# A weight load cut by rows: one 128-row transfer becomes four of 96, 25, 5 and 2 rows

## The chip, the core and the metric

The kernel runs on one core of a Trainium2 chip. The metric is the device time of one execution in microseconds (us), the median of several. The core has a matrix engine (TensorE, PE; its weight loads are shown as PEld), VectorE (DVE), ScalarE (ACT), GpSimd (POOL), SyncE (SP, which here only issues transfers and waits), and sixteen DMA engines that move data between the chip's main memory and the on-chip memory of 128 rows (partitions).

## The reference

One decoding step for 8 sequences, all in float32. `x` (8 by 512) is layer-normalised. Attention over a cache with 32 query heads and 8 key/value heads of 128, 4096 positions each, gives `o` (8 by 4096); the output projection multiplies it with `wo` (4096 by 512). A small gated MLP on the same normalised `x` gives a gate. The result is

```
s = softmax(q k^T / sqrt(128)) v  @ wo        # 8 x 512
out = x + s * silu(mlp(xn))                   # 8 x 512
```

The key and value caches are 128 MB each; `wo` is 8 MB.

## The kernel before, in words

All large operands come in transfers of 8 MB, 128 rows of 64 KB, into three slots of on-chip memory, `slot_a`, `slot_b` and `slot_c`. Per key/value head there are four: two halves of the keys (slots a and b) and two halves of the values (slots c and b). SP issues all of them in `Heads.loads`, in the order written there, each after a wait on TensorE's progress that says the slot is free. After the last head, slot a takes `wo` instead of the next keys.

`wo` comes in seven pieces, cut along the columns of the slot (`WO_PIECES`, in units of 256 columns, 1 KB of each row). Every piece has a semaphore of its own in `landed_wo`; a transfer adds 16 to it when all of it has landed. A piece's transfer has 128 rows, one for each partition. The sixth piece, units 60 to 63, has 3 KB a row. The small table `x_out` (128 rows of 256 bytes, the residual in the output's layout) is issued last.

`last_products` is the end of TensorE's program. It multiplies the attention output of the first seven heads with their part of `wo` (line 415, 56 products into two banks, `part`). Then VectorE and ScalarE copy these partial sums to on-chip memory (`part_sb`). TensorE meanwhile multiplies two of the last head's four parts (`direct`, line 424), folds the copied sums in (line 437), and multiplies the last two parts (line 424 again), into one bank `acc`. `need(column)` places a wait for a piece ahead of the first product that reads it, in the order of the program: the fifth piece (units 56 to 60) ahead of the first products of line 424, the sixth ahead of the ones that follow line 437, the seventh (unit 63 alone) ahead of the last quarter of those. A wait takes the semaphore down again:

```
    def take(self, sem, n):
        self.nc.tensor.wait_ge(sem, n).then_inc(sem, -n)
```

Behind the last product VectorE multiplies `acc` with the gate and adds `x_out` (two operations on 128 by 64), and ScalarE's queue issues the store of the result (32 KB).

Of the kernel before, what the change touches and what calls it, by code (L numbers as in the profile page):

```python
# [10 lines left out]
P = 128  # L11
# [13 lines left out]
SLOT = HALF * UNIT  # L25
W = 64
OUT_ROWS = 2 * B
WO_PIECES = [(0, 36), (36, 46), (46, 52), (52, 56), (56, 60), (60, 63), (63, 64)]
FOLDED = HKV * REP - REP
AHEAD = FOLDED + 2  # L30
HD = 256
# [7 lines left out]
class Chip:  # L39


    def __init__(self, nc):
        self.nc = nc

        def sb(name, *shape):
            return nc.alloc_sbuf_tensor(name, list(shape), F32).ap()
# [23 lines left out]
        self.oT = sb("oT", P, HKV - 1, REP, B)  # L70
        self.oT_last = sb("oT_last", P, REP, 2, OUT_ROWS)
        self.o_sb = [sb(f"o_sb{i}", P, DH) for i in range(2)]
# [158 lines left out]
class Heads:  # L231
# [7 lines left out]
    def __init__(self, nc, t, landed_a, landed_b, stored):  # L239
# [3 lines left out]
        self.landed_a, self.landed_b, self.landed_c = landed_a, landed_b, nc.alloc_semaphore("landed_c")  # L243
        self.landed_wo = [nc.alloc_semaphore(f"landed_wo{i}") for i in range(len(WO_PIECES))]
        self.landed_x = nc.alloc_semaphore("landed_x")
# [24 lines left out]
    def loads(self, kT, v, wo, x_rows):  # L270
        sync, (a, b, c) = self.nc.sync, self.t.slots
        for h in range(HKV):
            at = h * STEPS
            if h:
                sync.wait_ge(self.pe, at - 8 + 7)
                sync.dma_start(b, kT[h, 1]).then_inc(self.landed_b, 16)
                sync.wait_ge(self.pe, at - 8 + 6)
            sync.dma_start(c, v[h, 0]).then_inc(self.landed_c, 16)
            sync.wait_ge(self.pe, at + 2)
            sync.dma_start(b, v[h, 1]).then_inc(self.landed_b, 16)  # L280
            sync.wait_ge(self.pe, at + 1)
            if h < HKV - 1:
                sync.dma_start(a, kT[h + 1, 0]).then_inc(self.landed_a, 16)
        for (lo, hi), landed in zip(WO_PIECES, self.landed_wo):
            sync.dma_start(a[:, lo * HD:hi * HD], wo[:, lo * HD:hi * HD]).then_inc(landed, 16)
        sync.dma_start(self.t.x_out, x_rows).then_inc(self.landed_x, 16)

    def head_sides(self, h):
# [103 lines left out]
    def last_products(self):  # L392
        nc, t, step = self.nc, self.t, lambda mm: mm.then_inc(self.pe, 1)
        wo_sb = t.slots[0].rearrange("p (m d) -> p m d", d=D)
        half_d = D // 2
        here = [0]
        self.idle_products()

        def need(column):
            while here[0] < len(WO_PIECES) and WO_PIECES[here[0]][0] < column:  # L400
                self.take(self.landed_wo[here[0]], 16)
                here[0] += 1

        def quarter(m, i):
            return 2 * (m % 2) + i if m >= FOLDED - 2 else m % REP

        last = {(i, quarter(m, i)): m for m in range(FOLDED) for i in range(2)}
        starts = sorted({*range(0, FOLDED, REP), *(lo // 2 for lo, _ in WO_PIECES if lo < 2 * FOLDED), FOLDED})
        for lo, hi in zip(starts, starts[1:]):
            for i in range(2):  # L410
                for m in range(lo, hi):
                    need(2 * m + 2)
                    h, r = divmod(m, REP)
                    q = quarter(m, i)
                    mm = nc.tensor.matmul(self.part[i][R * q:R * q + B, :], t.oT[:, h, r, :],
                                          wo_sb[:, m, i * half_d:(i + 1) * half_d],
                                          start=(m < REP), stop=(m == last[i, q]))
                if hi == FOLDED:
                    step(mm)

        def direct(m, a, c, stop=False):
            need(2 * m + 2 if m < HKV * REP - 1 else 2 * m + 1 + a)
            for g in range(G):
                mm = nc.tensor.matmul(t.acc[R * g:R * g + OUT_ROWS, :], t.oT_last[:, m - (HKV - 1) * REP, a, :],  # L424
                                      wo_sb[:, m, c(g):c(g) + W], start=(m == FOLDED and a == 0), stop=stop)
            return mm

        self.take(self.token, 1)
        for m in range(FOLDED, AHEAD):
            for a in range(2):  # L430
                direct(m, a, lambda g: (2 * g + a) * W)
        self.take(self.token, 1)
        self.take(self.part1, 1)
        for a in range(2):
            for g in range(G):
                c = (2 * (g % 2) + a) * W
                nc.tensor.matmul(t.acc[R * g:R * g + OUT_ROWS, :], t.pick[:, a, :OUT_ROWS],  # L437
                                 t.part_sb[g // 2][:, c:c + W], start=False, stop=False)
        for m in range(AHEAD, HKV * REP):
            for a in range(2):  # L440
                if m < HKV * REP - 1:
                    direct(m, a, lambda g: (2 * g + a) * W)
                else:
                    mm = direct(m, a, lambda g: (G * a + g) * W, a == 1)
        step(mm)
# [55 lines left out]
```

## Time and profile before

| | us |
|---|---|
| median of 3 runs (678.39 to 678.44) | 678.40 |
| the profiled execution's own time | 678.71 |
| its span, first to last instruction | 677.4 |
| TensorE busy (modelled ends) | 405.8 |
| VectorE busy | 80.0 |
| ScalarE busy | 13.8 |
| main DMA queue, share of sixteen engines' span | 99.3% |

The span is the profiled execution on the one core; its own time holds what lies around the span too. A product's end is modelled, so a busy TensorE isn't TensorE at its peak. The DMA share of a window counts packets by when they begin and can pass 1 in a short one.

### The profile page before, as it was taken

Reading aid. Unit: us, or ns where it says so; the run is one execution under the profiler, and the core shown is the slowest. Engines: PE = TensorE matmul, PEld = TensorE weight load, DVE = VectorE, ACT = ScalarE, POOL = GpSimd, SP = SyncE. Lnnn points to the kernel's source line nnn. Section 1 sums busy time; section 2 is a strip of 40 time slices with the busy share of each in tenths; the row PEclk is TensorE's granted clock in tenths of the full one; section 3 lists DMA queues with packets and bytes.
Section 4 is the critical chain, followed back from the end, with each engine's and each line's share of the span. In section 5 each row is a group of like instructions: output and inputs, shape, how many; then the busy total and the mean of one; then the engine's idle time right before and its main releaser. Section 6 shows DMA issues by size and latency. Waiting matters only on the chain. (4 is left out here: it accounts for less than half of the span.)

```text
span 677.4 us, 5930 instructions
## 1 busy us (share of the span) xinstructions
PE 405.8 (60%) x2660; PEld 133.2 (20%) x2660; DVE 80.0 (12%) x157; ACT 13.8 (2%) x28; POOL 2.8 (0%) x15
## 2 busy tenths in 40 slices
PE   0446749346875449445794349555593349655598
PEld 0112213111221113111231113111131013211134
DVE  0142021102110021102110021101100021100211
ACT  0010000000000000000000000000000000000000
POOL 1000000000000000000000000000000000000000
PEclk9986869787896669788796779877696788976699
DMA  9999999999999999999999999999999999999997
GB/s 379 443 433 434 434 434 433 434 433 433 433 433 433 433 433 433 433 433 433 433 433 433 433 433 433 433 433 433 433 433 433 433 433 433 433 433 433 433 444 304
DMA packets 6213, 290.89 MB, mean 429 GB/s; under 512 B 952, under 2 KB 1080, under 8 KB 1600
## 3 DMA queue, kind: packets, MB, share of 16 engines
q1 hardware_dynamic: 6064, 290.79, 99.3%
q8 instruction: 4, 0.07, 0.0%
q10 hardware_dynamic: 144, 0.03, 0.0%
q14 instruction: 1, 0.01, 0.0%
HBM read 290.78 MB, written 0.03 MB: 429 GB/s over the span
## 5 line engine op out<-in xcount | busy, mean ns | idle before, releaser
L358 PE MATMUL sc<-slot_b,q 128*32 128x512 f32 x512 | 72.8, 733 | 75.8 <-PEq L340 75.8
L358 PE MATMUL sc<-slot_a,q 128*32 128x512 f32 x512 | 71.8, 724 | 72.4 <-PEq L340 72.4
L380 PE MATMUL o_ps<-slot_c,pT 128*16 128x512 f32 x512 | 72.4, 729 | 50.8 <-PEq L340 50.8
L373 PE MATMUL scr<-pT,ident 128*128 128x512 f32 x176 | 77.7, 597 | 0.0
L380 PE MATMUL o_ps<-slot_b,pT 128*16 128x512 f32 x512 | 56.5, 593 | 5.0 <-PEq L340 4.9
L358 PEld LDWEIGHTS sc<-slot_b,q 128*32 128x32 f32 x512 | 20.5, 132 | 128.2 <-issue 128.2
L264 DVE TENSOR_REDUCE nm<-sc 128x1 f32<-128x1024 f32 x8 | 9.8, 1224 | 290.1 <-PE sc L358 290.1
L358 PEld LDWEIGHTS sc<-slot_a,q 128*32 128x32 f32 x512 | 19.9, 131 | 117.9 <-issue 117.9
L373 PEld LDWEIGHTS scr<-pT,ident 128*128 128x128 f32 x176 | 32.8, 190 | 45.1 <-issue 45.1
L380 PEld LDWEIGHTS o_ps<-slot_c,pT 128*16 128x16 f32 x512 | 17.2, 112 | 99.4 <-issue 99.4
L380 PEld LDWEIGHTS o_ps<-slot_b,pT 128*16 128x16 f32 x512 | 15.7, 97 | 45.0 <-issue 45.0
L264 DVE TENSOR_TENSOR p<-o_ps,diag 128x512 f32<-128x512 f32 x8 | 5.5, 691 | 124.4 <-PE o_ps L380 124.4
L295 ACT ACTIVATE p<-sc,nm 128x1024 f32<-128x1024 f32 x8 | 8.9, 1114 | 554.3 <-DVE nm L264 554.3
L264 DVE TENSOR_TENSOR o_all<-o_ps,diag 128x512 f32<-128x512 f32 x8 | 5.5, 691 | 104.6 <-PE o_ps L380 104.6
L143 PE MATMUL scr<-ident,slot_c 8*128 8x8 f32 x4 | 0.6, 254 | 25.2 <-DVE slot_c L140 25.2
L345 PE MATMUL scr<-pT,ident 128*128 128x384 f32 x36 | 13.8, 507 | 0.0
L151 PE MATMUL scr<-slot_b,xnT 128*32 128x512 f32 x64 | 9.9, 779 | 0.3 <-DVE xnT L144 0.3
L262 DVE STREAM_TRANSPOSE pT<-p 128x1024 f32<-128x1024 f32 x8 | 10.0, 1245 | 0.3
L362 PE MATMUL scr<-ident,nm 128*1 128x128 f32 x8 | 2.2, 269 | 11.9 <-PEq L340 11.9
L262 DVE TENSOR_REDUCE o_sb<-p 128x128 f32<-128x512 f32 x8 | 8.3, 1033 | 0.3
L262 DVE TENSOR_REDUCE o_sb<-o_all 128x128 f32<-128x512 f32 x8 | 8.3, 1032 | 0.3
L388 PEld LDWEIGHTS po<-fold,o_sb 128*128 128x128 f32 x32 | 4.8, 188 | 13.5 <-issue 13.5
(96 smaller groups left out, 100.3 us busy)
## 6 DMA issues: line engine op xcount, KB each, us to landing
slot_c<-in_w_mlp SPq DMA_DIRECT2D x1, 5392.0 KB, 34.0
slot_a<-in_wo SPq DMA_DIRECT2D x1, 4608.0 KB, 39.2
slot_a<-in_wo SPq DMA_DIRECT2D x1, 1280.0 KB, 41.7
slot_a<-in_wo SPq DMA_DIRECT2D x2, 512.0 KB, 44.7
slot_a<-in_wo SPq DMA_DIRECT2D x1, 768.0 KB, 43.1
slot_a<-in_wo SPq DMA_DIRECT2D x1, 384.0 KB, 45.4
slot_a<-in_kT SPq DMA_DIRECT2D x8, 48.6
slot_b<-in_kT SPq DMA_DIRECT2D x8, 31.4
```

The lines of the kernel that those rows point to most:

```text
L143: nc.tensor.transpose(pt[:, k * B:(k + 1) * B], xn[:, k * P:(k + 1) * P], t.ident[:B, :B])
L151: nc.tensor.matmul(pq[R * g:R * (g + 1), :], t.xnT[:, k, :], wq_sb[:, k, lo:lo + REP * DH], start=(k == 0), stop=(k == NK - 1))
L262: make(*args, **kw).then_inc(self.token, 1)
L264: make(*args, **kw).then_inc(self.dve, 1)
L295: nc.scalar.activation(p, t.sc.rearrange("p c s -> p (c s)"), AF.Exp, bias=t.nm, accum_out=t.l).then_inc(self.act, 1)
L345: self.nc.tensor.matmul(t.scr[1][:, :WARM], t.ident, t.pT.rearrange("p j b g r -> p (j b g r)")[:, :WARM], start=True, stop=True)
L358: mm = nc.tensor.matmul(t.sc[R * g:R * (g + 1), c, :], t.q[:, b * R:(b + 1) * R], k_sb[:, i, c, g, :], start=(b == 0), stop=(b == B - 1))
L362: step(nc.tensor.transpose(t.scr[0][:1, :P], t.nm, t.ident))
L373: nc.tensor.matmul(t.scr[1], t.ident, flat[:, :512], start=True, stop=True)
L380: mm = nc.tensor.matmul(of[R * i:R * i + G * REP, :], pT[:, j, half * HALF + i], v_sb[:, i, j], start=(j == 0), stop=(j == J - 1))
L388: mm = nc.tensor.matmul(t.po[:, half * n:(half + 1) * n], t.o_sb[half], t.fold.rearrange("p i r -> p (i r)"), start=True, stop=True)
```

## The change

The sixth piece of `wo` is issued as four transfers, over rows 0 to 96, 96 to 121, 121 to 126 and 126 to 128, all into the same columns as before and all on the same semaphore; the wait for this piece asks for 64 in place of 16. The other pieces, the order of the pieces, and everything else stay.

```
+SHARED_PIECE = 5
+SHARES = [(0, 96), (96, 121), (121, 126), (126, 128)]
...
-        for (lo, hi), landed in zip(WO_PIECES, self.landed_wo):
-            sync.dma_start(a[:, lo * HD:hi * HD], wo[:, lo * HD:hi * HD]).then_inc(landed, 16)
+        for i, ((lo, hi), landed) in enumerate(zip(WO_PIECES, self.landed_wo)):
+            for p0, p1 in SHARES if i == SHARED_PIECE else [(0, P)]:
+                sync.dma_start(a[p0:p1, lo * HD:hi * HD], wo[p0:p1, lo * HD:hi * HD]).then_inc(landed, 16)
...
-                self.take(self.landed_wo[here[0]], 16)
+                self.take(self.landed_wo[here[0]], 16 * (len(SHARES) if here[0] == SHARED_PIECE else 1))
```

## Rows read from the trace of the kernel before

**Rows 1.** The page: DMA share and rate by slices, queue's packets, MB, share.

```profile
span 677.4 us, 5930 instructions
...
DMA  9999999999999999999999999999999999999997
GB/s 379 443 433 434 434 434 433 434 433 433 433 433 433 433 433 433 433 433 433 433 433 433 433 433 433 433 433 433 433 433 433 433 433 433 433 433 433 433 444 304
...
q1 hardware_dynamic: 6064, 290.79, 99.3%
```

**Rows 2.** Timeline of SP's last issues (start us, us, instruction).

```profile
626.34 0.33 SPq L280 DMA_DIRECT2D slot_b<-in_v  x1
626.71 3.28 SPq L285 DMA_DIRECT2D slot_a<-in_wo  x7
630.03 17.23 SPq L286 DMA_DIRECT2D x_out<-in_x_rows  x1
```

**Rows 3.** DMA issues from 629.0 to 629.2 us (KB each, us to landing).

```profile
slot_a<-in_wo SPq DMA_DIRECT2D x1, 512.0 KB, 45.0
slot_a<-in_wo SPq DMA_DIRECT2D x1, 384.0 KB, 45.4
```

**Rows 4.** DMA issues of the whole span (KB each, median us to landing).

```profile
slot_a<-in_wo SPq DMA_DIRECT2D x1, 4608.0 KB, 39.2
...
slot_a<-in_wo SPq DMA_DIRECT2D x1, 128.0 KB, 45.3
x_out<-in_x_rows SPq DMA_DIRECT2D x1, 32.0 KB, 45.0
out<-gate ACTq DMA_DIRECT2D x1, 32.0 KB, 1.5
...
slot_c<-in_x SPq DMA_DIRECT2D x1, 16.0 KB
```

**Rows 5.** Timeline of the end (start us, us, engine, instruction, idle before).

```profile
673.69 0.49 PEld L424 LDWEIGHTS acc<-slot_a,oT_last 128*16 128x16 f32 x32 [0.95 <-issue]
673.72 0.64 PE L424 MATMUL acc<-slot_a,oT_last 128*16 128x64 f32 x32 [0.48 <-PEq L340]
674.11 0.30 PEld L437 LDWEIGHTS acc<-part_sb,pick 128*16 128x16 f32 x16
674.17 0.42 PE L437 MATMUL acc<-part_sb,pick 128*16 128x64 f32 x16
674.60 0.54 PEld L424 LDWEIGHTS acc<-slot_a,oT_last 128*16 128x16 f32 x32 [0.18 <-issue]
674.63 0.68 PE L424 MATMUL acc<-slot_a,oT_last 128*16 128x64 f32 x32
675.35 0.22 DVE L264 TENSOR_TENSOR gate<-acc,gate 128x64 f32<-128x64 f32 x1 [1.65 <-PE acc L424]
675.61 0.22 DVE L264 TENSOR_TENSOR gate<-gate,x_out 128x64 f32<-128x64 f32 x1
675.86 0.37 ACTq L335 DMA_DIRECT2D out<-gate  x1
```

**Rows 6.** Chain that ended last, in order of time (start us, us).

```profile
673.68 0.04 issue
673.72 0.64 PE acc L424 x32
...
674.59 0.04 issue
674.63 0.70 PE acc L424 x26
```

**Rows 7.** Windows of the end, with PEclk, DMA share and GB/s last.

```profile
672.80:673.30 0.50, 0.44 (x8) 0.00 (x0) 0.03 (x1) 0.00 (x0) 0.00 (x0) 1.00 0.84 280
673.30:673.60 0.30, 0.00 (x0) 0.00 (x0) 0.30 (x1) 0.27 (x1) 0.00 (x0) 1.00 0.38 137
673.60:674.20 0.60, 0.48 (x35) 0.51 (x39) 0.10 (x1) 0.10 (x1) 0.00 (x0) 1.00 0.28 101
674.20:674.60 0.40, 0.39 (x28) 0.22 (x17) 0.00 (x0) 0.00 (x0) 0.00 (x0) 1.00 0.13 31
674.60:675.40 0.80, 0.68 (x32) 0.53 (x32) 0.05 (x1) 0.00 (x0) 0.00 (x0) 1.00 0.00 0
```

**Rows 8.** DMA queues from 669 to 677.4 us: packets, MB, share.

```profile
q8 instruction: 1, 0.02, 0.7%
```

## The prediction

> **What bounds the kernel now.** I read the page's slices and queue lines first, then the chain of waits, the timeline of the last six microseconds, the windows of the same stretch, and last the DMA issues with their landings.
>
> The page says that the kernel lives on its loads: one queue moves 290.79 MB and its packets fill 99.3% of sixteen engines' time [rows 1]. So the body runs at the pace of the transfers, and only what comes after the last load, or an uneven end of the loads, is open. The change touches only that end.
>
> The landings follow from issue plus time to landing. SP issues the seven pieces of wo from 626.71 in 3.28 us, one each 0.474 us, and x_out at 630.03 [rows 2]. The fifth piece (512 KB) is issued at 626.71 + 4 x 0.474 = 628.61 and lands 45.0 later, at 673.6; the sixth (384 KB, the one that is cut up) at 629.08 + 45.4 = 674.5 [rows 3]; the seventh (128 KB) at 629.55 + 45.3 = 674.9; x_out at 630.03 + 45.0 = 675.0 [rows 4].
>
> TensorE shows two of these as stops. Its weight loads for the folded tail begin at 673.69, 0.1 us after the fifth piece, and those of the last 32 products at 674.60, 0.1 us after the sixth [rows 5]. The view of the chain makes the stretch from 673.72 to 675.32 look like unbroken TensorE work, with 0.04 us of "issue" in it [rows 6]. But a product's end there is modelled. The weight loads tell more: those of line 437 are over at 674.11 + 0.30 = 674.41, and the next is at 674.60 with 0.18 us of idle before it [rows 5]. **So TensorE waits 0.18 us for the piece that is changed**, and no more than that can be won by landing it sooner: ahead of it stands work that the fifth piece released, and the change doesn't touch the fifth piece.
>
> The other thing to see is why the end is ragged. The DMA share is 0.84 from 672.80 to 673.30, then 0.38, 0.28 and 0.13 until 674.60 [rows 7]. Times 16 that is 6.1, then 4.5, then 2.1 engines' worth of data. If all sixteen finished together the share would fall in one step. So some eleven engines are through at about 673.3, and four or five run on, the slowest until the landing at 674.5. After 669 one 16 KB packet of instructions passes too, on another queue [rows 8]; it takes one engine for a while, and whatever that engine owes of wo is later by that much. A landing waits for the last engine.
>
> **The change part by part.** *Three more issues on SP.* An issue takes 0.43 us and one starts each 0.474 us [rows 2]: 3 x 0.474 = 1.4 us, at about 630 us. Nothing but the seventh piece and x_out stands behind them, both due 43 us later. One stall is visible: x_out's own issue lasts 17.23 us, to 647.26 [rows 2], as if the engines' queues had to drain first. With 17 packets for this piece on the fullest engine in place of 9 (below), eight more must drain before x_out fits. The first piece of wo (4,608 KB, 36 KB a row, landing at 626.71 + 39.2 = 665.9 [rows 4]) needs 4,719 / 434 = 10.9 us at the page's 434 GB/s [rows 1], so it begins at 655; even if all eight were its rows (1.36 us each), x_out is issued by 655 + 8 x 1.36 = 665.9. Its data pass at 674.5 or so: hidden by over 8 us, and without that cover VectorE's last sum at 675.61 [rows 5] would wait for it. Bounds: 0 to 0; a loss would need over 8 us more.
>
> *The wait.* TensorE still takes one semaphore once, of 64 instead of 16; no instruction is added. Zero.
>
> *Who carries the rows.* A row of this piece costs an engine (674.5 - 673.6) / 8 = 0.11 us, since the piece lands 0.9 us behind the one before it and eight rows per engine lie between; 3 KB at 434 / 16 = 27 GB/s gives 0.113, the same. The queue's 6,064 packets [rows 1] tell how transfers are cut: 128-row ones (42 of them) in 16 equal parts with one completion each, 42 x 144 = 6,048, and the 8-row transfer of x [rows 4] leaves 16, eight rows and eight completions, so eight engines with a row each. If 25, 5 and 2 rows are cut into equal parts likewise, they go to 5, 5 and 2 engines, and 96 rows to 16 engines of six. If the small ones begin at the same engine, two engines carry 13 rows, three carry 12, eleven carry 6, in place of 8. The eleven are through 2 x 0.11 = 0.22 us sooner, the five 0.44 to 0.55 later. The trace doesn't show where 25 rows go; its bounds are sixteen engines (no shift) and one engine (below). I take five.
>
> [...]
>
> *What it is worth.* If the four or five late engines are all among the eleven, the piece lands at 674.5 - 0.22 = 674.28, TensorE could go on at 674.39, and its loads are free at 674.42: the 0.18 us are gone. The seventh piece then lands 0.22 sooner too (674.64), and the last quarter of the products, which needs it, comes at about 674.42 + 0.75 x 0.54 = 674.83. So the sum is -0.18 us against the profiled execution, whose 678.71 us hold the span of 677.4 and 1.3 around it. The median of the runs is 0.31 below that execution; the same difference gives **678.40 - 0.18 = 678.2 us**.
>
> **The rivals.** *One of the late engines is among the five.* The five then finish 0.55 later, and it is a late one that does. If it is the slowest, the piece lands at 674.5 + 0.55 = 675.05 and everything behind follows: 678.95 us. If it is one of the others, which by the fall of the share are through by about 674.2 [rows 7], it lands at 674.75: 678.65. For it: rows of views name no engine, and five of sixteen are a large part. Against: what ends last is one engine, and 11 of 16 places are outside the five. It decides from the point where a late engine that carries 12 or 13 rows was less than 0.55 us ahead of the slowest.
>
> *It doesn't do what it says*: the small transfers spread over all engines and nothing shifts. 678.4 us.
>
> *25 rows stay on one engine.* With 5 and 2 on the same, it carries 38 rows, 30 more than now: 30 x 0.11 = 3.3 us. From an engine that was through at 673.2 that is 676.5, 2.0 us later than now: 680.4 us, or 681.7 from the slowest. Against it: the 8-row transfer used as many engines as it could.
>
> *Small transfers pay a fixed cost one after the other.* The final store of 32 KB takes 1.5 us from issue to landing with nothing else in flight [rows 4]; three times that would be 4.5 us, 682.9 us. Against it: x_out, also 32 KB, lands 0.1 to 0.2 us behind the piece before it [rows 4], so behind other work that time is overlapped. [...]
>
> **How the numbers follow.** The slowest engine falls outside the five with 11/16 = 0.69 if nothing is known of its place; the other late ones take some of that away. All late engines outside the five 0.48 (678.2); nothing shifts 0.07 (678.4); a late one among the five 0.18 (678.65), or the slowest 0.20 (678.95); one engine for 25 rows 0.04; fixed costs 0.02; something that gains more 0.01. The range 678.0 to 679.1 holds the first four, 0.93. 0.2% is 1.36 us, about what a measurement of this kernel can tell from no change; the first four lie inside it on both sides, so same 0.93, slower 0.06, faster 0.01.
>
> **What would show it.** The queue has 6,064 + 5 + 5 + 2 = 6,076 packets if 25, 5 and 2 rows go to 5, 5 and 2 engines (the completions of the 96 rows stand for those of the 128), 6,064 + 1 + 5 + 2 = 6,072 if the 25 stay on one, 6,064 + 48 = 6,112 if each goes to all sixteen. The idle time ahead of the last 32 products is gone or a few hundredths if I am right; 0.4 to 0.8 us, with the share of 673.6 to 674.6 higher, if a late engine is among the five. x_out's issue ends before 666. The loads for the folded tail still begin 0.1 us behind the fifth piece, at about 673.7. I am wrong if that moves, if the body before 655 runs at another pace, or if the time leaves 678.0 to 679.1.

## The result and the profile after

The changed kernel takes 679.60 us (median of 21 runs) against 678.48 us of the kernel before (21 runs of the same sessions): the ratio is 1.0016, with an interval of 1.0009 to 1.0022, so 0.6 to 1.5 us slower. That is under the 0.2% (1.36 us) that the prediction took for what a measurement can tell from no change, though by its interval it is a real loss. It lies outside the prediction's range (678.0 to 679.1), and it moved the other way.

The page of the changed kernel, its main queue:

```profile
q1 hardware_dynamic: 6076, 290.79, 99.2%
```

6,076 packets are what 25, 5 and 2 rows on 5, 5 and 2 engines give. The rows go to as many engines as forecast; which ones, no row names.

The timeline of SP in the changed kernel, answering to [rows 2]:

```profile
626.70 14.03 SPq L288 DMA_DIRECT2D slot_a<-in_wo  x10
640.78 14.54 SPq L289 DMA_DIRECT2D x_out<-in_x_rows  x1
```

The issues of the pieces now stall too, but x_out is issued at 640.78 + 14.54 = 655.3, 17 us before the first of its packets begins (672.40, by the packet records). Nothing waits for SP.

The timeline of the end in the changed kernel, answering to [rows 5]:

```profile
674.26 0.49 PEld L427 LDWEIGHTS acc<-slot_a,oT_last 128*16 128x16 f32 x32 [1.84 <-issue]
...
675.49 0.54 PEld L427 LDWEIGHTS acc<-slot_a,oT_last 128*16 128x16 f32 x32 [0.51 <-issue]
...
676.24 0.23 DVE L266 TENSOR_TENSOR gate<-acc,gate 128x64 f32<-128x64 f32 x1 [2.87 <-PE acc L427]
```

Two stops grew. The loads that wait for the **fifth** piece, which the change leaves whole, begin at 674.26 instead of 673.69 [rows 5]: +0.57. From there to the loads that wait for the sixth it is 1.23 us instead of 0.91: +0.32. The sum, 0.89, is the whole difference of the two profiled executions (679.60 against 678.71). By the idle time in front of them (the brackets) the two stops grew by 0.89 and 0.33; the changed execution had come to this point 0.33 us earlier. Behind it everything keeps its length.

Why the fifth piece is late shows in windows of the same stretch (DMA share and GB/s are the last two columns). The changed kernel:

```profile
671.90:672.40 0.50, 0.34 (x8) 0.13 (x8) 0.00 (x0) 0.00 (x0) 0.00 (x0) 1.00 1.16 248
672.40:672.90 0.50, 0.50 (x8) 0.02 (x4) 0.00 (x0) 0.00 (x0) 0.00 (x0) 1.00 0.91 199
```

And the kernel before:

```profile
671.90:672.40 0.50, 0.35 (x5) 0.00 (x0) 0.00 (x0) 0.00 (x0) 0.00 (x0) 1.00 0.96 391
672.40:672.90 0.50, 0.27 (x8) 0.15 (x8) 0.00 (x0) 0.00 (x0) 0.00 (x0) 1.00 1.00 388
```

Read the two columns together. From 672.40 to 672.90 the engines are about as busy (0.91 against 1.00), but move 199 GB/s instead of 388. Not fewer engines work: a packet takes about 1.8 times as long (388 / 1.00 against 199 / 0.91). The trace also keeps a record of each packet, which no view lists. Of the packets that begin in this half microsecond, the 3 KB ones of the cut piece took 121 ns each before and 212 on average after the change; the 4 KB ones of the fifth piece, 159 and 276. So the late engines, still at the fifth piece, are slowed too. The drop begins at about 671.9; the cut piece's first packet begins at 671.1, and 55 of the 56 that begin ahead of 671.9 still take 121 ns. Why these pass unhindered stays open.

### The profile page after: what moved, and what is told of

Its sections match the earlier page's. It is cut to its first block, busy times and chain, and to the rows that moved or that the text cites. A ratio compares the mean times of both kernels' runs of the same rounds, so it can differ in the third digit from the quotient of the medians.

```text
span 678.3 us, 5933 instructions
## 1 busy us (share of the span) xinstructions
PE 408.1 (60%) x2660; PEld 133.6 (20%) x2660; DVE 80.0 (12%) x157; ACT 13.8 (2%) x28; POOL 2.8 (0%) x15
## 3 DMA queue, kind: packets, MB, share of 16 engines
q1 hardware_dynamic: 6076, 290.79, 99.2%
```

## The experiments

Four theories were held against each other: L, a late engine is among the five with more rows (the prediction's main rival); F, each added transfer costs by itself; D, rows that reach other destination rows than an engine has in a 128-row transfer make the engines hinder each other; and later S, that it is the source rows. C, at the first piece, is F once more. All times are medians against the kernel before on the same chip.

**Four transfers, cut along the columns.**

```
+            n = N_PARTS if i == SHARED_PIECE else 1      # 4
+            w = (hi - lo) * HD // n
+            for k in range(n):
+                at = slice(lo * HD + k * w, lo * HD + (k + 1) * w)
+                sync.dma_start(a[:, at], wo[:, at]).then_inc(landed, 16)
```

> The sixth piece in four transfers, each of all 128 rows and a quarter of its columns. Theory F (each added transfer costs by itself): about as the change, +0.9 to +1.1 us against the kernel before. Theory L (a late engine is among the five that carry more rows): no engine carries more, 0 within 0.2 us. Theory D (rows that go to other destination rows than an engine has in a 128-row transfer make engines hinder each other): every transfer has the usual cut, 0 within 0.2 us.

678.66 against 678.48 us, ratio 1.0003 (0.9994 to 1.0012). Its rate in the slow stretch of the change:

```profile
672.40:672.90 0.50, 0.39 (x8) 0.00 (x0) 0.08 (x1) 0.02 (x1) 0.00 (x0) 1.00 1.03 348
```

Four transfers of 768 bytes a row, with 48 more completions by the prediction's count of 16 a transfer, cost 0.18 us, with an interval of -0.4 to 0.8. F, which asked for 0.9 to 1.1, is out.

**96 and 32 rows, without uneven shares.**

```
+SHARES = [slice(0, 96), slice(96, 128)]
...
+            for rows in SHARES if i == SHARED_PIECE else [slice(0, P)]:
+                sync.dma_start(a[rows, lo * HD:hi * HD], wo[rows, lo * HD:hi * HD]).then_inc(landed, 16)
```

> The sixth piece as 96 and 32 rows: six and two rows for each of sixteen engines, eight in all as before, but cut elsewhere. F: a third of its cost, about +0.3 us. L: 0 within 0.2 us, since no engine carries more than before. D: packets of the stretch after 672 take longer on all engines, as in the changed kernel, the fifth piece lands later too, and +0.5 to +1.3 us.

679.31 against 678.48, ratio 1.0012 (1.0003 to 1.0021): +0.83 of the change's +1.12 us, though each engine has eight rows as before, if these transfers too are cut into sixteen equal parts. The same cut of the first piece, below, has 6,080 packets, 16 completions more, which fits. Its window shows the same drop, and its timeline the same late fifth piece (674.58 in place of 673.69):

```profile
672.40:672.90 0.50, 0.29 (x4) 0.00 (x0) 0.00 (x0) 0.00 (x0) 0.00 (x0) 1.00 1.03 227
```

```profile
674.58 0.49 PEld L427 LDWEIGHTS acc<-slot_a,oT_last 128*16 128x16 f32 x32 [1.50 <-issue]
```

**64 and 64 rows.** The same lines with `SHARES = [slice(0, 64), slice(64, 128)]`.

> The sixth piece as 64 and 64 rows: four rows twice for each of sixteen engines. F: +0.3 us. L: 0 within 0.2 us. D: each transfer reaches half of the rows with all the engines, so they hinder each other for its whole length; a piece of 0.9 us at up to twice the time is +0.5 to +1.0 us.

679.66 against 678.48, ratio 1.0022 (1.0013 to 1.0032): +1.18 us, about what the change costs and somewhat over D's +0.5 to +1.0. Again balanced by the same count (6,080 packets for this cut of the first piece), again slow: uneven shares are not needed for the loss.

**The same extra load on as many engines, without on-chip rows.**

```
+            if i == SHARED_PIECE:
+                for p0, p1 in EXTRA:                      # (96, 121), (121, 126), (126, 128)
+                    sync.dma_start(self.spare[p0:p1], wo[p0:p1, lo * HD:hi * HD]).then_inc(self.landed_x, 16)
```

> The sixth piece whole, in one transfer of 128 rows; ahead of it the 25, 5 and 2 rows are copied once more, from main memory to a spare buffer in main memory, on the semaphore of x_out. The same engines carry seven or six extra rows, none leaves the others, and no on-chip row is touched. L: the sixth piece lands later by 6 or 7 rows of 0.11 us, +0.6 to +0.8 us. D: the sixth piece lands as before unless a late engine is among the five, 0 within 0.2 us. F: +0.9 to +1.1 us.

678.55 against 678.48, ratio 1.0001 (0.9992 to 1.0010). Its queue shows that the extra rows went to as many engines as in the change: 6,064 + 32 rows + 5 + 5 + 2 completions = 6,108. Its timeline shows the two stops, 0.93 us apart as before (0.91):

```profile
q1 hardware_dynamic: 6108, 290.88, 99.3%
```

```profile
673.39 0.49 PEld L430 LDWEIGHTS acc<-slot_a,oT_last 128*16 128x16 f32 x32 [1.24 <-issue]
...
674.32 0.54 PEld L430 LDWEIGHTS acc<-slot_a,oT_last 128*16 128x16 f32 x32 [0.21 <-issue]
```

The packet records show that the extra rows weren't free: all 160 packets of 3 KB, copies and piece alike, took 121 ns. Which engines had the copies no view shows; if the three transfers begin at the same engine, as the prediction assumed, five had six or seven rows more. The piece didn't land later, so at this price none of the engines with that many copies decides its end. If the change's extra rows go to the same engines, L is out: the late engines that matter are among the others, which is the case that the prediction took as likeliest. Without that assumption too, 64 and 64 rows lose as much as the change with no engine given more.

**The 96 rows alone.** `SHARES = [slice(0, 96)]`.

> Only rows 0 to 96 of the sixth piece are loaded, in one transfer; rows 96 to 128 of these columns keep what the slot held, so a quarter of this piece's data is left out. Each engine has six rows, as the eleven have in the change. Theory D (engines that write the same places hinder each other): the 96 rows alone do it; the fifth piece still lands late, and in spite of the missing data the time is 0 to +0.8 us. Rival: the small transfers do it and the cut of 96 is harmless; then the piece lands two rows sooner and the time is -0.2 us.

678.79 against 678.50, ratio 1.0004 (0.9995 to 1.0013). With a quarter of the piece gone no gain is seen. By the time alone the rival's -0.2 us stays possible (the interval is -0.3 to 0.9). The trace speaks for D: the rate is down as in the change, and the loads behind the fifth piece begin at 673.98, after 1.78 us of idle in place of 0.95 [rows 5]:

```profile
672.40:672.90 0.50, 0.30 (x8) 0.00 (x0) 0.17 (x1) 0.11 (x1) 0.00 (x0) 1.00 1.05 217
```

```profile
673.98 0.50 PEld L427 LDWEIGHTS acc<-slot_a,oT_last 128*16 128x16 f32 x32 [1.78 <-issue]
```

So the 96-row transfer by itself is enough to bring the rate down, from 388 to 217 GB/s, for its neighbours above all: in this half microsecond a packet of the fifth piece took 267 ns in place of 159. That the 32 rows then add to the loss isn't shown: 96 and 32 rows and 96 alone differ by 0.54 us, less than their intervals are wide.

**The shares first, the 96 rows last.**

> The four transfers of the change with the 96 rows last. D: the same data go to the same places from the same engines, so +0.7 to +1.4 us, like the change. If it is the small transfers at the end of the row that are late, the order helps: 0 to +0.4 us.

679.22 against 678.50, ratio 1.0010 (1.0001 to 1.0019): +0.72, in D's span at its lower end. Its interval (0.1 to 1.3) also holds the 0.4 of the other theory, and the difference to the change (0.4 us) is smaller than the intervals are wide. Whether the order helps a little stays open.

**The same cuts, twelve times as large.** The first piece of wo (4,608 KB) is cut instead of the sixth, where the transfers alone set the pace, so that the effect can be measured well outside the noise. A place, in theory D, is the set of destination rows that one engine has to itself in a 128-row transfer; which rows these are, no view shows. Before, the rate in this stretch is 413 GB/s:

```profile
657.00:665.00 8.00, 7.75 (x62) 2.95 (x51) 2.01 (x4) 0.00 (x0) 0.00 (x0) 1.00 0.96 413
```

64 and 64 rows (`SHARED_PIECE = 0`):

> The first piece of wo (4,608 KB, 36 KB a row, 10.9 us at the usual rate) as 64 and 64 rows, the sixth whole: the same cut as in the 64-and-64 run, 12 times as many bytes, in a place where the transfers alone set the pace. Theory D (destination rows): 64 rows in one half are written by all sixteen engines, two to each place that takes a row at full rate, so half the rate, 21.7 us, and about +10.9 us against the kernel before. Theory C (only the cut into more and smaller transfers costs, a fixed amount): under +1 us.

96 and 32 rows:

> The first piece of wo as 96 and 32 rows. [...] C: under +1 us.

Eight times 16 neighbouring rows (`slice(k * 16, (k + 1) * 16)`):

> The first piece of wo as eight transfers of 16 rows that lie next to each other, one row for each engine. [...] C: some +2 us for seven more transfers. Theory S (it is the source rows in main memory that collide): slower too, by the same amount as the next run.

Eight times 16 rows, from the same source rows, to every eighth destination row:

```
+SHARES = [slice(k, P, 8) for k in range(8)]
+FROM = [slice(k * 16, (k + 1) * 16) for k in range(8)]
...
+                sync.dma_start(a[rows, lo * HD:hi * HD], wo[src, lo * HD:hi * HD]).then_inc(landed, 16)
```

> The same as the run of eight times 16 rows, from the same 16 neighbouring source rows each time, but to every eighth destination row (the host arranges these columns of wo so that the result stays the same). [...] S and C: the same time as that run.

| cut of the first piece | median, us | before, us | difference | ratio, interval |
|---|---|---|---|---|
| 64 + 64 | 694.75 | 678.70 | +16.1 | 1.0240 (1.0223 to 1.0257) |
| 96 + 32 | 693.87 | 678.70 | +15.2 | 1.0234 (1.0217 to 1.0251) |
| 8 x 16 neighbouring | 709.24 | 678.70 | +30.5 | 1.0475 (1.0431 to 1.0519) |
| 8 x 16, every eighth | 693.58 | 678.70 | +14.9 | 1.0230 (1.0213 to 1.0247) |

The windows of these four in the table's order, one line from each:

```profile
657.00:673.00 16.00, 12.29 (x76) 4.20 (x76) 2.01 (x4) 0.00 (x0) 0.00 (x0) 0.89 0.94 194
```

```profile
657.00:673.00 16.00, 11.74 (x76) 3.76 (x68) 2.01 (x4) 0.00 (x0) 0.00 (x0) 0.91 1.04 221
```

```profile
657.00:673.00 16.00, 13.50 (x76) 4.14 (x76) 2.01 (x4) 0.00 (x0) 0.00 (x0) 0.79 1.02 124
```

```profile
657.00:673.00 16.00, 13.23 (x76) 4.14 (x76) 2.01 (x4) 0.00 (x0) 0.00 (x0) 0.81 1.00 207
```

All four keep sixteen engines busy (0.94 to 1.04) at 194, 221, 124 and 207 GB/s instead of 413. For one busy engine that is 13, 13, 8 and 13 GB/s instead of 27. The packet records agree: each of the piece's 128 packets took 1,364 ns before, and on average 2,892, 2,690, 4,680 and 2,851 in these four runs. The last two runs settle where it happens: the same source rows, the same number of transfers, packets and bytes, only other destination rows, and the loss is +14.9 instead of +30.5 us. S and C ask for the same time in both, so neither is the cause by itself; the destination rows decide. That no part of the +14.9 comes from the source rows isn't shown. Against the 10.9 us that the prediction works out for this piece, eight times 16 neighbouring rows take 10.9 + 30.5 = 41.4 us, nearly four times as long (a quarter of the rate would be 43.5); every eighth row takes 25.8 and 64 and 64 rows 27.0, somewhat over twice as long (half the rate would be 21.7). Why neighbouring rows lose twice as much as every eighth (+30.5 and +14.9), and which destination rows are slow together, these runs don't show; that two engines come to each place with 64 rows was the author's estimate.

Not all of each difference belongs to the loads. The first products on the piece, which begin at 666.00 in the kernel before, begin at 679.70 with 64 and 64 rows, 13.7 later, while the profiled span is 15.6 longer (693.0 against 677.4):

```profile
666.00 0.15 PEld L415 LDWEIGHTS sc<-slot_a,oT 128*8 128x8 f32 x8 [0.64 <-issue]
```

```profile
679.70 0.15 PEld L418 LDWEIGHTS sc<-slot_a,oT 128*8 128x8 f32 x8 [10.40 <-issue]
```

```profile
681.00:683.00 2.00, 2.00 (x24) 0.80 (x20) 0.00 (x0) 0.00 (x0) 0.00 (x0) 0.50 1.01 421
```

TensorE, which had waited some 10 us for the piece, then works at a granted clock of 0.50 until about 685 (0.86 from 685 to 687), and no later piece stops it any more: it is busy in all of the 8 us from 681 to 689. In the other three runs the first products begin 12.7, 29.4 and 13.9 us later. Counted to there, 64 and 64 rows take 24.6 us and every eighth row 24.8, still more than the 21.7 of half the rate, and 16 neighbouring rows 40.3.

The 64-and-64 run missed its expectation (+10.9 for a measured +16.1). How 96 rows are dealt to the engines is in no view, and why 96 and 32 rows (+15.2) are about as slow as 64 and 64 stays open.

**One engine to a place, by theory D.** Sixteen transfers of eight rows, every fourth row of a block of 32:

```
+SHARES = [slice(b + j, b + j + 29, 4) for b in range(0, P, 32) for j in range(4)]
```

> The first piece of wo as sixteen transfers of eight rows, every fourth row of a block of 32, so that only eight engines work, each on a row of its own place in every transfer. Theory D in the form that a place takes a row at the pace of one engine and two engines on it are slower than one: eight engines on eight places need 16 rows each at the full pace of an engine, 21.7 us, +10.9 us, less than the +14.9 and +16.1 of sixteen engines on eight places. If two on a place only share it: the same +15. Theory C (each added transfer costs): fifteen more transfers, more than the eight of 16 rows to every eighth row cost, over +15 us.

690.51 against 678.31, ratio 1.0176 (1.0159 to 1.0193): +12.2 us. That the eight rows of a transfer lie on eight places was the author's assumption. The queue's 6,176 packets are 112 completions more than 6,064, eight for each of sixteen transfers in place of sixteen for one, so eight engines carry each. A window of the stretch in which the share is down to a half:

```profile
666.00:676.00 10.00, 0.00 (x0) 0.00 (x0) 0.00 (x0) 0.00 (x0) 0.00 (x0) 0.73 0.49 209
```

Half of the engines busy at 209 GB/s is 27 GB/s for each, the pace of the kernel before, and by the packet records each of the 128 packets took 1,364 ns, as before. The first products on the piece begin at 676.75, 10.7 us later, and +10.9 would be the number of engines alone. So these eight don't hinder each other. Twice as many transfers on half as many engines are faster than 8 x 16 rows on sixteen (+14.9), which speaks against C once more. Sixteen engines are no faster than eight: the piece takes sixteen 128 x 2.851 / 16 = 22.8 us with every eighth row, and eight 128 x 1.364 / 8 = 21.8 us here. That the sixteen share eight places is theory D's reading of their half rate; no view shows it. The two runs differ in their source rows too, and no run separates that.

## Why the prediction was wrong, point by point

- *What bounds the kernel, the two stops, the 0.18 us of wait.* Right as read. The sentence "the change doesn't touch the fifth piece" failed: its instructions are untouched, but four or five engines, by the prediction's own reading, still carry its rows when the others start the cut piece, and their packets take 276 ns in place of 159. +0.57 us of the profiled 0.89 come from there.
- *Three more issues, the stall of SP, the wait for 64.* Right: x_out is issued at 655.3, and four transfers by columns cost 0.18 us, inside their interval.
- *Who carries the rows.* Right in count: 6,076 packets; that the three small transfers begin at the same engine, so that five engines carry more, no view shows. **The step that failed is the price**: "a row of this piece costs an engine 0.11 us", taken from a 128-row transfer and used for any row on any engine. A row's price hung on which destination rows were written: a 36 KB row of the first piece took 1,364 ns in one transfer, 4,680 to 16 neighbouring rows at a time and 2,851 to every eighth. With the sixth piece's rows cut otherwise the rate falls from 388 to 199 GB/s, and a row that begins there takes 212 ns in place of 121 (158 on average over the whole piece).
- *What it is worth.* The 0.22 us that the eleven engines were to save are taken by slower packets; even with a quarter of the piece left out no gain is seen (+0.3 us, its interval -0.3 to 0.9).
- *The rivals.* The late engine among the five, given 0.38 in all, is refuted by the extra load (+0.07 us), if its copies went to the same five. 25 rows on one engine and fixed costs in series are refuted by the packets and by the columns. The cause of the loss was not among the rivals.
- *The range.* All its cases moved rows between engines at a fixed price, so its upper end was one engine's five rows (0.55 us) and came out 0.5 us too low.
- *Left open*: how much of the change's +1.12 us is the 96-row cut and how much the shares. 96 and 32 rows give +0.83, 96 alone +0.29 without a quarter of the data, 64 and 64 +1.18; these intervals are about 0.6 us either way. Which engine writes which rows is in no view, and the small piece's first packets pass at the usual price.

## What to carry to other kernels

In this kernel a load of 4,608 KB ran at 413 GB/s in one transfer of 128 rows and at 124 to 221 GB/s when it was cut by rows, while a load of 384 KB cut along the columns cost 0.18 us, inside the noise. So when a transfer into on-chip memory has to be cut, try the columns first. Moving rows from late to early engines gained nothing here (+1.12 us): the cut by rows that it needs costs about as much with the engines' shares left even (+0.83 and +1.18 us). And when the price of a thing is read from one shape of transfer, the same bytes in another shape are a new price: look for a row of that shape, or make the range wide enough for half the rate.

## What was not expected of the hardware

The DMA share does not show the loss: it stays at 0.91 to 1.05 while the rate falls to 199 to 227 GB/s, because the share counts the time that packets take, and the packets took longer (212 ns for 3 KB in place of 121 in the change). Of the two columns only the rate tells. The small extra transfers themselves were cheap: 48 more completions and three more issues cost 0.18 us with an interval that holds zero, and 32 rows copied between two places in main memory, 0.07.
